# Longformer attention and cosine-gated layers on one Trainium2 core: seven products of quarters for the second layer of tiles 3 to 5, with new step lists

## The chip, the core and the metric

The kernel runs on one core of a Trainium2 chip. A core has TensorE (PE) for matrix products, with its weight loads shown apart (PEld), VectorE (DVE), ScalarE (ACT), GpSimd (POOL) and SyncE (SP), which issues DMAs. Each engine works through its own list of instructions in order, and waits on semaphores that other engines raise. The matrix products land in PSUM, eight banks of 128 partitions x 512 fp32 numbers. The metric is device time in microseconds (us), median over executions. One further execution is recorded by the hardware profiler, and all lines of the profile come from that one.

## What is computed

Attention over 8 batches of 8 heads with 576 positions and 64 numbers per head, where a position sees those at most 32 away, and 8 global positions see all and are seen by all; then two layers with a cosine gate between them.

```python
scores = scale * np.matmul(q, k.transpose(0, 1, 3, 2))
mask = np.abs(pos[:, None] - pos[None, :]) <= window
mask = mask | is_global[:, None] | is_global[None, :]
...
attn = np.exp(scores); attn = attn / (np.sum(attn, axis=-1, keepdims=True) + 1e-09)
x = np.matmul(attn, v).transpose(0, 2, 1, 3).reshape(B * S, H * D)   # 4608 x 512
h = x @ w_in                                                        # 512 x 2048
g = h * np.cos(h)
return g @ w_out                                                    # 2048 x 512
```

Inputs and output are fp32; products take fp16 operands.

## The kernel before

**Attention.** Two heads of one batch make a pair, so there are 32 pairs, four to a batch. A pair goes through these stations: local keys and queries copied beside the global ones (DVE, L630 and L642; the global ones by POOL, L600 and L607), scores (PE, L722, 22 small products into three PSUM banks `s` and one of `h`), exponentials (ACT, L725 for two blocks of 128x512, L730 for two rests of 128x192), mask products (DVE, L726 and L731), values (PE, L742, into `pv`), the division (DVE, L747 to L753), six transposes (PE, L767, into `tx`) and two copies into `xT` (DVE, L769 and L770). `x_squares` (ACT, L914) and, per batch, copies of the global rows (POOL, L775) follow.

**Layers.** The 4608 tokens are nine tiles of 512. A first-layer unit (`mlp_in`, L788) is four 512-column products into one bank `ph`; ACT takes the cosine (L794) and DVE multiplies (L795) into `g`. There are 16 such units to a tile. The second layer of tiles 0 to 5 is done directly: 16 units of four 512-column products (L892), a bank `po` copied out after every four units by ACT (L897) and DVE (L899) in turn, and stored. Tiles 6 to 8 (`WT = 6`) use seven products of quarter matrices in place of eight (`win`, L852): 14 units of eight 256-column products, with sums of quarters of `g` made ahead (`g_sum`, L822, eight DVE instructions of 1024 columns to a tile) and of `w_out` (`w_out_sum`, L808, eight in all), and results collected from two banks X and Y, by ACT copies where a result's first part comes, and DVE additions (L876) where its second does.

**Order.** The program writes each engine's order out by hand: a list of letters is run in sequence, and each letter appends its instructions to the engines. Steps s = 4 to 15 each treat two pairs, `a` (2s) and `z` (2s+1), and copy keys and queries for the next two, `c` and `d`. In a list, `1` is a first-layer unit with cosine and product, `2` a second-layer unit, `sa`/`sz` scores with exponentials and masks, `pa`/`pz` values with division, `xa`/`xz` transposes with their copies, `k.`/`q.` the local copies, `n` the squares, `J` one `w_out_sum`, `G` the casts: POOL copies the four global blocks, waits for the division of `z` through a small gate copy, and then issues three DMAs that write the fp16 v, k and q of step s+2 to DRAM. At the end of a step `bring(s + 2)` puts the transposing loads of keys and queries (SP, L295 and L296) and the value loads on SP's queue. `FRONT`, `MID` (s = 4), `FIFTH`, `SIXTH`, `ORDER` (s = 7 to 14), `LASTR` (s = 15) and `TAIL` are the lists. Each step of `ORDER` has eight `1` and eight `2`.

The two functions of ACT, exp and sine, need different tables; a table load stands before the first exponential and before the first cosine of each step.

Of the kernel before, what the change touches and what calls it, by code (L numbers as in the profile page):

```python
# [51 lines left out]
TAIL = "x0 a4 a5 o x1 a6 i w o i i o o i o w i w a7 o i w i o i v0 b0 o b1 i i o i o b2 i i o o w i w w i b3 o o i w b4 i o i b5 i o b6 w o i o i w o i v1 i o i w w o c0 b7 o i c1 v2 i o c2 i o c3 o i o i i w w o w i o i w o c4 c5 c6 o o c7 o v3 o F o o o o R o o o o o"  # L52
# [3 lines left out]
FIFTH = "sa G 2 2 2 n3 2 sz pa U10 K7 1 1 2 xa pz 2 2 2 kc qc xz n"  # L56

SIXTH = "kz qz sa 2 2 2 2 sz pa 1 2 1 2 xa n pz D0 1 1 G 2 xz 1 D1 1 2 kc qc 1 D2 1"
# [5 lines left out]
WT = 6  # L64
WIN = "1265734"
# [146 lines left out]
def kernel(  # L212
# [20 lines left out]

    ident = const.tile([P, P], FP32)
# [91 lines left out]
    def warm(n, tag="s"):  # L326

        t = ps.tile([P, 4, P], FP32, tag=tag, bufs=2 + (tag == "s"))
        for _ in range(n):
            nc.tensor.matmul(t, ones16, view(ones16, (0, 4), (1, P)), start=True, stop=True)  # L330
# [94 lines left out]
    def value_rows(s, part):  # L425

        hs = slice(2 * part, 2 * part + 2)
        rows = ps.tile([P, 512], FP32, tag="h", bufs=2, name="rows")
# [143 lines left out]
    def turn_globals(half, both):  # L572
        t = ps.tile([P, 2, 16 * G], FP16, tag="s" if half else "h", bufs=2 + half)
# [22 lines left out]
    def globals_k(pr):  # L596
        if pr < 2 * HY:
            nc.gpsimd.tensor_copy(k5(pr)[:, :, 0:G], view(kgT[:, pr], (0, NK5), (1, G)))
            return
        nc.gpsimd.tensor_copy(kw[pr % NK][:, :, 0:G], view(kgT[:, pr], (0, NB), (1, G)))  # L600

    def globals_q(pr):
# [4 lines left out]
        nc.gpsimd.tensor_copy(qp[:, :, 0:G], view(qgT[:, pr], (0, NB), (1, G)))  # L607

    def turned(src, pr, n, ahead=0):

        bank = ps.tile([P, 512], FP32, tag="h", bufs=2, name="bank")
        for _ in range(ahead):
            nc.tensor.matmul(bank, ones16, view(ones16, (0, 4), (1, P)), start=True, stop=True)
        t = view(bank.bitcast(FP16), (QP, RW), (1, QP))
# [4 lines left out]
        return t, bank[:, 400 : 400 + G]  # L619
# [23 lines left out]

    def scores5(pr):
        kp, qp = k5(pr), qb[pr % NK].rearrange("p j c -> p (j c)")
        pm = pm_of[pr] = work.tile([P, 2 * CN], FP16, tag="pm", name="pm")
        tags = (("s", 3), ("s", 3), ("s", 3), ("o", 1))
        st = [ps.tile([P, 512], FP32, tag=tag, bufs=bufs, name="st") for tag, bufs in tags]
# [44 lines left out]
    def turn_x5(pr, tag="s"):  # L693
        b, p = pr // NP, pr % NP
# [4 lines left out]
        tx = ps.tile([P, NK5, P], FP16, tag=tag, bufs=2 + (tag == "s"))  # L699
# [12 lines left out]
    def scores(pr):  # L712
        if pr < 2 * HY:
            return scores5(pr)
        kp, qp = kw[pr % NK], qb[pr % NK]
        pm = pm_of[pr] = view(work.tile([P, 2 * CN], FP16, tag="pm", name="pm"), (NB * C, 2), (C, NB), (1, C))
        tags = (("s", 3), ("s", 3), ("s", 3), ("o", 1) if front[0] else ("h", 2))
        st = [ps.tile([P, 512], FP32, tag=tag, bufs=bufs, name="st") for tag, bufs in tags]
        for j in range(NB):
            for h in range(2):  # L720
                hp = slice(h * D, (h + 1) * D)
                nc.tensor.matmul(st[j // 8 * 2 + h][:, j % 8 * C : j % 8 * C + C], kp[hp, j], qp[hp, j], start=True, stop=True)  # L722
        for h in range(2):
            e = work.tile([P, 2 * CB], FP16, tag="e", bufs=3)
            nc.scalar.activation(e[:, 0:512], st[h], AF.Exp, scale=scale)  # L725
            nc.vector.tensor_tensor(view(pm[:, h], (1, 512)), e[:, 0:512], view(mask, (1, 512)), ALU.mult)  # L726
        e = work.tile([P, 2 * CB], FP16, tag="e", bufs=3)
        n = (NB - 8) * C
        for h in range(2):
            nc.scalar.activation(e[:, h * n : (h + 1) * n], st[2 + h][:, 0:n], AF.Exp, scale=scale)  # L730
        nc.vector.tensor_tensor(view(pm[:, 0, 8], (NB * C, 2), (1, n)), view(e, (n, 2), (1, n)), view(mask[:, 8], (0, 2), (1, n)), ALU.mult)  # L731

    def values(pr):
        if pr < 2 * HY:
            return values5(pr)
        pm, vp = pm_of.pop(pr), vw[pr % NV]
        for j0 in range(0, NB, 2):
            for h in range(2):
                for j in range(j0, min(j0 + 2, NB)):
# [3 lines left out]
                                     start=True, stop=True)  # L743
        den = pv[:, :, D : D + 1]
# [11 lines left out]

    def turn_x(pr):
        if pr < 2 * HY:
            return turn_x5(pr, "h" if 5 < pr < 8 else "s")
        b, p = pr // NP, pr % NP  # L760
        xn = xn_of[pr // 2][:, pr % 2]
        if p == 0:
            xg_of[b] = work.tile([P, NP, G], FP16, tag="xg", name="xg")
        xg = xg_of[b]
        tx = ps.tile([P, BP, P], FP16, tag="s", bufs=3)
        for n in range(BP):
            nc.tensor.transpose(tx[:, n], xn[:, n], ident16)  # L767
# [9 lines left out]
    def mlp_in(t, f):  # L777
# [6 lines left out]
        else:  # L784
            ph = ps.tile([P, TT], FP32, tag=tag, bufs={"s": 3, "h": 2}[tag], name="ph")
# [12 lines left out]
    w_of = [xT[:, :, i * TT : (i + 1) * TT] for i in range(4)]  # L798
# [11 lines left out]
    s_of, wp_of, o_of, o_next = {}, {}, {}, [0]  # L810

    def g_sum(t, k):

        n, part = HF // 4, k // 4
        if t not in s_of:
            s_of[t] = [room[3]] + [xT[:, :, i * TT : (i + 1) * TT] for i in (4, 5)] if t % 2 else room[0:3]
        s1, s2, s4 = (x[:, n * part : n * part + n].rearrange("p a (b n) -> p a b n", n=NH) for x in s_of[t])
# [12 lines left out]
    def win(t, u):  # L830

        name, a = WIN[u // 2], u % 2
        g16, wo = g_of[t], w_out16
        s1, s2, s4 = s_of[t] if t in s_of else (None,) * 3
        half = lambda x, f: x[:, f // 2, f % 2 * NH : f % 2 * NH + NH]
        left = {"1": lambda f: g16[:, f, 0:NH], "2": lambda f: g16[:, HF + f, 0:NH], "3": lambda f: half(s4, f),
                "4": lambda f: g16[:, HF + f, NH:], "5": lambda f: half(s1, f), "6": lambda f: half(s2, f),
# [7 lines left out]
        if name == "1" and (split or a == 0):  # L845
            tag = "h" if split else "o"
            X[at] = ps.tile([P, 2, NH], FP32, tag=tag, bufs={"h": 2, "o": 1}[tag], name="wx")
        if name in "25" and (split or a == 0):
            Y[at] = ps.tile([P, 2, NH], FP32, tag="s", bufs=3, name="wy")
        bank = (X if name in "1674" else Y)[at]  # L850
        for f in range(HF):
            nc.tensor.matmul(bank[:, a], left(f)[:, a * P : a * P + P], right(f),  # L852
# [4 lines left out]
        b = bank[:, cols]  # L857
        if name == "1" and cols.start == 0 or name == "1" and not split:
            o_of[t] = [o_room() for _ in range(4)]
        o11, o12, o21, o22 = (o[:, cols] for o in o_of[t])  # L860
# [4 lines left out]
        if name == "1":  # L865
            nc.scalar.copy(o11, b)
        elif name == "6":
            nc.scalar.copy(o12, b)
        elif name == "5":
            nc.scalar.copy(o22, b)  # L870
        elif name == "4":
            nc.scalar.copy(o21, b)
            store(o21, 1, 0, nc.scalar if split else nc.sync)
        else:
            o, tok, col = {"2": (o11, 0, 0), "3": (o12, 0, 1), "7": (o22, 1, 1)}[name]
            nc.vector.tensor_tensor(o, b, o, ALU.add)  # L876
            if not split or name != "2":
                store(o, tok, col, nc.sync)
            elif a:
                store(o_of[t][0], tok, col, nc.sync)  # L880

    def mlp_out(t, u):
# [4 lines left out]
        if part == 0:  # L887
            tag = "s" if (tail[0] or spare[0]) and s % 2 else "o"
            po_of[t] = ps.tile([P, DM], FP32, tag=tag, bufs={"s": 3, "o": 1}[tag], name="po")
# [37 lines left out]
    def weight_norms(c):  # L927
        sq = w_sq.pop(c)
        pn = ps.tile([P, 512], FP32, tag="s", bufs=3)
# [27 lines left out]
    def raise_flag(count):  # L957
        tot, onesf = count
        pt = ps.tile([P, 512], FP32, tag="o", bufs=1)
# [6 lines left out]
    outs_q = [(t, u) for t in range(NTT) for u in range(NF if t < WT else 2 * len(WIN))]  # L966
# [20 lines left out]
    outs_by = [0]  # L987
# [12 lines left out]
    with tc.manual_schedule():  # L1000
# [36 lines left out]
        pv = ps.tile([P, 2, 512], FP32, tag="pv", bufs=1)  # L1037
# [35 lines left out]
        def casts(s):  # L1073

            for pr in (2 * s + 2, 2 * s + 3):
                if pr < B * NP:
                    globals_kq(pr)
# [8 lines left out]
        def bring(s):  # L1086
# [6 lines left out]
        OTHER = LOCAL | {"g": globals_kq, "L": load_qk, "W": load_w_in, "v": load_values, "n": x_squares,  # L1093
                 "C": cast_vn, "I": row_numbers, "E": early_rows, "w": lambda n: warm(n, "h" if n == 6 else "s"), "y": value_rows, "M": next_values, "S": spread_vg, "V": hold, "N": hold_mask, "U": hold_x, "H": early_globals, "Z": steady_buffers, "f": fill, "r": load_vn, "A": later_rows, "D": later_globals, "O": load_w_out, "K": lambda s: cast_half(s, "kqv"), "B": bring, "J": w_out_sum, "j": lambda k: g_sum(WT, k), "m": lambda _: one(False), "t": lambda _: mlp_act()}
# [8 lines left out]
        for s in range(4, B * NP // 2):  # L1103
            outs_by[0] = 8 * (s - 3)
            for step in {4: MID, 5: FIFTH, 6: SIXTH, 15: LASTR}.get(s, ORDER).replace("J", f"J{s - 7}" if s < 15 else "").split():
# [10 lines left out]
                elif step == "n":  # L1116
                    x_squares(s - 1)
                elif step == "R":
# [75 lines left out]
```

## Time and profile before

| what | value |
|---|---|
| median of three runs | 337.71 us (337.55 to 337.84) |
| the profiled execution | 339.82 us |
| its span | 338.1 us |
| mean granted clock of TensorE | 0.986 |
| DVE, ACT, POOL busy, share of the span | 80%, 71%, 32% |

The span runs from the first to the last instruction of the profiled execution; 1.7 us of that execution lie outside it. A busy share is an average over the whole span: the program has a front of 80 us (loads, the first eight pairs), the steps up to about 266 us, and a tail of tiles 7 and 8. From 76 us to the last slice but one the page's slices show PE at 9 (90% or more). From 300 us on, only layers are left.

### The profile page before, as it was taken

To read this page: it belongs to the slowest core of one execution; us is meant where nothing else is said; L and a number is where in the kernel's file an instruction comes from. 1 tells how busy PE (TensorE), PEld (TensorE's weight loads), DVE (VectorE), ACT (ScalarE), POOL (GpSimd) and SP (SyncE) were. 2 spreads that over 40 slices of the span, in tenths; PEclk is the share of its full clock that TensorE was granted. 3 is DMA by queue.
4 is the path that set the end of the run, shared out by engine and by line. 5 is a ranking of instruction groups with operands and counts; after the bars stand their busy time and mean duration, and the time that the engine had idled before them with its cause. 6 is when DMAs were issued, how large, how long until landed. Compare 5 with 4: busy or idle time off the path is not lost.

```text
span 338.1 us, 8637 instructions
## 1 busy us (share of the span) xinstructions
PE 325.8 (96%) x3269; PEld 182.1 (54%) x3269; DVE 271.8 (80%) x648; ACT 241.6 (71%) x423; POOL 107.2 (32%) x216
## 2 busy tenths in 40 slices
PE   7989989999999999999999999999999999999993
PEld 3567664444445454545454545454545566666682
DVE  6757998996488889889888989898889877778781
ACT  4776886786768787878787878787878775666720
POOL 6856567624061507060805080507000200000000
PEclk9996999999999999999999999999999999999998
DMA  4999899999999999999999999999990000200212
GB/s 74 209 166 179 162 204 202 196 148 149 143 137 180 131 161 146 176 141 172 154 200 139 202 131 185 136 181 148 209 112 34 32 33 0 95 32 0 94 47 86
DMA packets 167203, 45.00 MB, mean 133 GB/s; under 512 B 153092, under 2 KB 163716, under 8 KB 166980
## 3 DMA queue, kind: packets, MB, share of 16 engines
q1 hardware_dynamic: 107396, 26.60, 55.3%
q0 software_dynamic: 59472, 17.54, 53.1%
q8 instruction: 27, 0.44, 0.6%
q10 hardware_dynamic: 288, 0.26, 0.2%
q14 instruction: 20, 0.16, 0.2%
HBM read 44.93 MB, written 19.17 MB: 190 GB/s over the span
## 4 chain that ended last, share of the span: by engine, by line
PE 80%; DVE 7%; ACT 5%; issue 2%; DMA 2%; SPq 2%; POOL 0%; ACTq 0%; DVEq 0%
PE ph L788 27%; PE po L892 21%; PE wx L852 6%; PE wy L852 5%; PE units L788 4%; PE t L330 3%; PE pv L742 3%; PE st L722 2%; DVE g L795 2%; DMA vw<-vg 2%; PE tx L767 2%; PE bank L618 2%; PE pv L669 1%; PE st L654 1%; ACT cos L794 1%
## 5 line engine op out<-in xcount | busy, mean ns | idle before, releaser
L788 PE MATMUL ph<-xT,w_in 128*128 128x512 f16 x512 | 123.3, 379 | 0.4
L794 ACT ACTIVATE cos<-ph,pio 128x512 f16<-128x512 f32 x128 | 86.4, 686 | 41.9 <-PE ph L788 39.9
L795 DVE TENSOR_TENSOR g<-cos,ph 128x512 f16<-128x512 f16 x128 | 85.6, 683 | 18.0 <-ACT cos L794 16.2
L892 PE MATMUL po<-w_out,g 128*128 128x512 f16 x384 | 93.5, 379 | 0.0
L788 PEld LDWEIGHTS <-w_in 128*128 128x128 f16 x576 | 53.9, 98 | 57.5 <-issue 1.5
L892 PEld LDWEIGHTS <-g 128*128 128x128 f16 x384 | 36.6, 98 | 43.1
L725 ACT ACTIVATE e<-st 128x512 f16<-128x512 f32 x44 | 23.9, 594 | 8.2 <-PE st L722 8.1
L726 DVE TENSOR_TENSOR pm<-e,mask 128x512 f16<-128x512 f16 x44 | 18.8, 427 | 13.4 <-ACT e L725 12.1
L1079 POOL COPY gate<-xn 1x1 f16<-1x1 f16 x8 | 1.4, 179 | 81.4 <-DVE xn L753 81.4
L775 POOL COPY xT<-xg 128x4 f16 x48 | 15.9, 331 | 32.0 <-DVE xT L770 29.4
L281 POOL DMA_DIRECT2D q<-in_q_dram x11 | 24.3, 2206 | 0.0
L753 DVE TENSOR_TENSOR xn<-pv,r_all 128x768 f16<-128x768 f32 x22 | 21.1, 958 | 0.7
L852 PEld LDWEIGHTS <-g 128*128 128x128 f16 x192 | 18.7, 98 | 5.2
L914 ACT ACTIVATE xn<-xn 128x1536 f16<-128x1536 f16 (+1 forms) x15 | 21.2, 1411 | 0.0
L281 POOL DMA_DIRECT2D k<-in_k_dram x11 | 18.0, 1638 | 1.4 <-issue 1.4
L794 ACT ACTIVATE cos<-units,pio 128x512 f16<-128x512 f32 x16 | 11.0, 688 | 9.8 <-PE units L788 9.6
L795 DVE TENSOR_TENSOR g<-cos,units 128x512 f16<-128x512 f16 x16 | 11.0, 686 | 7.4 <-ACT cos L794 7.2
L788 PE MATMUL units<-xT,w_in 128*128 128x512 f16 x64 | 16.4, 379 | 0.0
L794 ACT ACT_TABLE_LOAD x12 | 15.4, 1283 | 0.2
L657 ACT ACTIVATE e<-st 128x488 f16<-128x488 f32 x20 | 10.4, 572 | 6.4 <-PE st L654 6.4
L725 ACT ACT_TABLE_LOAD x11 | 14.1, 1283 | 0.2
L600 POOL COPY kw<-kgT 128x88 f16<-128x88 f16 x22 | 14.0, 858 | 0.0
(214 smaller groups left out, 505.8 us busy)
## 6 DMA issues: line engine op xcount, KB each, us to landing
out_dram<-o SPq DMA_DIRECT2D x24, 256.0 KB
vw<-v SPq DMA_DIRECT2D x32, 165.0 KB
k<-in_k_dram POOLq DMA_DIRECT2D x11, 288.0 KB, 8.2
q<-in_q_dram POOLq DMA_DIRECT2D x11, 288.0 KB, 10.7
v<-in_v_dram POOLq DMA_DIRECT2D x11, 288.0 KB, 5.5
vn<-in_v_dram SPq DMA_DIRECT2D x20, 120.0 KB
w_in<-in_moe_w_in_dram POOLq DMA_DIRECT2D x4, 512.0 KB, 9.3
w_out<-in_moe_w_out_dram POOLq DMA_DIRECT2D x1, 2048.0 KB, 17.0
```

What stands on the lines that cost most here:

```text
L281: nc.gpsimd.dma_start(dst[s].rearrange("t (h d) -> t h d", h=4), dview(src, base, (D, S), (S * D, 4), (1, D)))
L600: nc.gpsimd.tensor_copy(kw[pr % NK][:, :, 0:G], view(kgT[:, pr], (0, NB), (1, G)))
L725: nc.scalar.activation(e[:, 0:512], st[h], AF.Exp, scale=scale)
L726: nc.vector.tensor_tensor(view(pm[:, h], (1, 512)), e[:, 0:512], view(mask, (1, 512)), ALU.mult)
L753: nc.vector.tensor_tensor(view(xn, (384, 2), (D, 6), (1, D)), view(pv, (512, 2), (65, 6), (1, D)), view(rp, (6, 2), (1, 6), (0, D)), ALU.mult)
L775: nc.gpsimd.tensor_copy(xT[:, :, bass.ds(pool_idx[g] + b * S, 1)], xg[:, :, g : g + 1])
L788: nc.tensor.matmul(ph, w_in16[:, j, f * P : (f + 1) * P], xT[:, j, t * TT : (t + 1) * TT], start=(j == 0), stop=(j == NC - 1))
L794: nc.scalar.activation(cos, ph, AF.Sin, bias=pio2)
L795: nc.vector.tensor_tensor(g, cos, ph, ALU.mult)
L852: nc.tensor.matmul(bank[:, a], left(f)[:, a * P : a * P + P], right(f), start=name in "125" and f == 0 and (split or a == 0), stop=f == HF ...
L892: nc.tensor.matmul(po, g16[:, f, s * P : (s + 1) * P], w_out16[:, f], start=(f == 0), stop=(f == NF - 1))
L914: nc.scalar.activation(view(xn, (BP * P, 2), (1, n)), view(xn, (BP * P, 2), (1, n)), AF.Square, accum_out=x_sq[:, s : s + 1])
```

## The change

1. **`WT = 3`:** tiles 3 to 5 take the seven products too, in the order 1, 2, 6, 7, 5, 3, 4. Their sums of `g` lie in columns of `xT` whose tokens are used up (`g_rooms`), the sums of `w_out` in `room`, made by `J0` to `J7` in steps 6 to 9, where before they came one a step in 7 to 14. Each of these tiles' outputs leaves as four quarters `oq`, four ACT copies and three DVE additions to a tile, in place of two ACT and two DVE copies.
2. **Banks:** the pools of PSUM become one tile `banks` of all eight banks, with a fixed ring for each purpose. From step 4 on, both score pairs of a step write banks 0, 1 and 2 (and one of the `h` banks 4 and 5). Transposes take banks 2 and 0 in turn; X of the seven products is bank 3 and Y bank 1.
3. **Smaller letters:** scores with exponentials (`e`), masks (`h`), values (`b`), division (`d`), transposes (`l`) and their copies (`u`) can be placed apart. The two 128x512 exponentials become one of 128x2x512 that writes `pm` at once; the masks are multiplied in place, 128x2x512 and 128x2x192.
4. **Tables:** `load_table` is a 1x1 ACTIVATE whose only use is that the table is loaded there: sine after the odd pair's exponentials, exp at the letter `P`.
5. **Globals:** for pairs 12 and up ACT, not POOL, copies the global keys and queries (`yc`, `yd`), four to a step.
6. **Lists:** `FIFTH` and `SIXTH` are rewritten, steps 7, 8 and 9 get lists of their own with eight `1` and eight `2` each, and from 10 on `EVEN` (six `1`, of them one as `m` and `t`, and five `2`) and `ODD` (ten and nine) alternate; step 15 has a new `LASTR`. `m` is a first-layer unit whose cosine and product wait for the letter `t`.

```diff
-ORDER = "2 kz qz sa 2 2 2 sz pa 1 2 1 2 xa n pz 1 1 G J 2 xz 1 1 2 kc qc 1 1"
-LASTR = "2 kz qz sa 2 2 2 sz pa 1 j0 2 1 2 xa n pz 1 1 j1 2 xz 1 j2 1 2 1 j3 1"
+SEVENTH = "2 kz ea qz 2 J4 2 ez ha 2 ba hz da 1 2 J2 1 bz dz la ua yd 2 n 1 G 1 2 lz uz kc 1 1 qc yc 2 1 1 J3"
...
+NINTH = "kz 2 ea qz 2 ha yc 2 2 ez hz ba da 1 2 1 2 n la ua bz yd dz 1 1 G 2 lz j0 J7 uz 1 1 qc kd kc 2 1 j1 1 qd"
+EVEN = "ea j4 2 j3 ha ez j5 m hz ba da t 2 kc 1 2 yd bz dz 1 1 la n ua 2 G yc qc 1 1 P lz uz j7 2 qd kd"
+ODD = "2 ea j2 2 ha j6 ez hz 2 ba da 1 1 2 bz la dz 1 1 ua G n 2 qd lz 1 1 yc 2 j0 uz 1 1 yd 2 kc 1 qc m 2 t P kd j1 2"
+LASTR = "2 ea j2 2 ha j6 ez hz 2 ba da 1 1 2 bz la dz 1 1 ua n 2 lz 1 1 2 j0 uz 1 1 2 2 1 2 j1 1"
...
-WT = 6
-WIN = "1265734"
+WT = 3
+WIN = "1265734", "1267534"
...
+    banks = ps.tile([P, 8, 512], FP32, tag="banks", bufs=1, name="banks")
+    rings, turns = {"s": [0, 1, 2], "o": [3], "h": [4, 5], "t": [2, 0], "y": [1]}, {}
...
+    def score_banks(pr):
+        return [bank(tag) for tag in "ssso"] if front[0] else [banks[:, i] for i in (0, 1, 2)] + [bank("h")]
...
+            nc.scalar.activation(both, banks[:, 0:2], AF.Exp, scale=scale)
...
+        if not front[0] and pr % 2:
+            load_table(AF.Sin)
+    def mask_scores(pr):
...
+        nc.vector.tensor_tensor(both, both, view(mask, (0, 2), (1, 512)), ALU.mult)
+        nc.vector.tensor_tensor(rest, rest, view(mask[:, 8], (0, 2), (1, n)), ALU.mult)
...
-        nc.gpsimd.tensor_copy(kw[pr % NK][:, :, 0:G], view(kgT[:, pr], (0, NB), (1, G)))
+        (nc.scalar.copy if pr > 11 else nc.gpsimd.tensor_copy)(kw[pr % NK][:, :, 0:G], view(kgT[:, pr], (0, NB), (1, G)))
...
+    def g_rooms(t, part):
+        if t < 6:
+            c = column((t if part else t - 2) % NTT)
+            return c[:, 0:2], c[:, 2:4], c[:, 2:4]
```

**Scores at a step's start.** On ACT, before, a step of `ORDER` begins behind the cosines of the last step (`cos`) with the table load (the kernel's L725) and the exponentials of `a` and `z`; on PE three second-layer units stand between the two pairs' scores.

```order
L794 ACTIVATE cos<-ph,pio_71 128x512 x2
L725 ACT_TABLE_LOAD
L725 ACTIVATE e<-st 128x512 x2
L730 ACTIVATE e<-st 128x192 x2
L725 ACTIVATE e<-st 128x512 x2
L730 ACTIVATE e<-st 128x192 x2
```

After, from step 11's end into step 12, the table load of `P` and its 1x1 instruction come ahead of a copy out of bank X (`oq<-banks`), and that copy ahead of the exponentials, which now write the masked products' place `pm`.

```order
L854 ACTIVATE cos<-banks,pio_72 128x512 x2
L746 ACT_TABLE_LOAD
L746 ACTIVATE table<-pio_72 1x1
L943 COPY oq<-banks 128x512
L762 ACTIVATE pm<-banks 128x2x512
L764 ACTIVATE pm<-banks 128x192 x2
L762 ACTIVATE pm<-banks 128x2x512
```

The copy, which frees bank X for the next second-layer unit, moved to the step's first place on ACT, and a cosine's table is left a unit earlier. On PE the same place reads, with waits: the last of one second-layer unit's products (L923), then the first scores of `z` (L756) with the semaphore of ACT, `Activation_49`.

```order
L923 LDWEIGHTS g
L923 MATMUL banks<-room_90,g 128x256
L756 LDWEIGHTS kw_100 [waits DVE_49]
L756 MATMUL banks<-qb_104,kw_100 128x64 [waits Activation_49]
L756 LDWEIGHTS kw_100
L756 MATMUL banks<-qb_104,kw_100 128x64
```

One unit of eight products stands there between the scores of `a` and of `z` in the steps of `EVEN` and `ODD`, where three units of four stood; `z` writes the banks that `a` wrote.

**DVE in a step.** Before, a step begins with the masks, a copy out of `po` between them, and the division.

```order
L726 TENSOR_TENSOR pm<-e,mask 128x512 x2
L731 TENSOR_TENSOR pm<-e,mask 128x2x192
L899 COPY o<-po 128x512
L726 TENSOR_TENSOR pm<-e,mask 128x512 x2
L731 TENSOR_TENSOR pm<-e,mask 128x2x192
L747 TENSOR_REDUCE dg<-pv 8x2
```

After, in a step of `EVEN`, sums of quarters (L892) stand ahead of and between the masks.

```order
L892 TENSOR_TENSOR xT<-xT,g 128x2x512
L892 TENSOR_TENSOR xT<-g 128x2x512
L892 TENSOR_TENSOR g<-g 128x4x256
L772 TENSOR_TENSOR pm<-pm,mask 128x2x512
L773 TENSOR_TENSOR pm<-pm,mask 128x2x192
L892 TENSOR_TENSOR xT<-xT,g 128x2x512
L772 TENSOR_TENSOR pm<-pm,mask 128x2x512
L773 TENSOR_TENSOR pm<-pm,mask 128x2x192
L797 TENSOR_REDUCE dg<-banks 8x2
```

The first of these sums ends the step of `ODD` before, the other three belong to `EVEN`; a tile's eight sums of 1024 columns are spread four to a step of either kind, where before there was one sum of `w_out` to a step. The copy out of `po` is gone from between the masks.

More of the change, by code (lines that the diff above doesn't have):

```diff
@@ L427, in value_rows @@
         hs = slice(2 * part, 2 * part + 2)
-        rows = ps.tile([P, 512], FP32, tag="h", bufs=2, name="rows")
+        rows = bank("h")
         for t in range(NK5):
@@ L797 @@
     NH, HF = DM // 2, NF // 2
-    w_of = [xT[:, :, i * TT : (i + 1) * TT] for i in range(4)]
+    w_of = room
     def w_out_sum(k):
```

174 lines of the change are left out of this document (98 added, 76 removed).

## Prediction

> **What bounds the kernel now.** I read the page's busy table first, then windows of 20 us, since a share over the whole span mixes stages.
>
> ```profile
> 80.00:100.00 20.00, 18.98 (x193) 9.39 (x192) 12.69 (x30) 13.12 (x22) 4.29 (x6) 1.00 1.40 153
> 120.00:140.00 20.00, 20.00 (x220) 10.37 (x220) 17.68 (x41) 15.88 (x26) 6.73 (x16) 1.00 1.55 164
> 200.00:220.00 20.00, 20.00 (x201) 10.01 (x199) 17.14 (x38) 16.39 (x27) 6.88 (x16) 1.00 1.70 159
> 240.00:260.00 20.00, 20.00 (x205) 10.34 (x204) 17.59 (x38) 16.12 (x26) 0.00 (x0) 1.00 0.89 113
> ```
>
> The columns are the window, its length, then busy us of PE, PEld, DVE, ACT and POOL, the granted clock, the DMA share and GB/s. In the steps PE is busy 20.00 of 20 at a clock of 1.00: PE is the bound, DVE follows at 86 to 88%, ACT at 80%. Only the window that holds step 5 leaves PE idle, 1.02 us. The timeline gives the period:
>
> ```profile
> 116.94 0.49 PE L722 MATMUL st<-qb,kw 64*128 64x64 f16 x22
> 117.37 2.76 PE L892 MATMUL po<-w_out,g 128*128 128x512 f16 x12
> ...
> 124.45 0.50 PE L767 MATMUL tx<-ident,xn 128*128 128x128 f16 x6
> 124.88 0.57 PE L742 MATMUL pv<-vw,pm 128*64 128x65 f16 x22
> ...
> 127.98 0.50 PE L767 MATMUL tx<-ident,xn 128*128 128x128 f16 x6
> 128.32 1.89 PE L788 MATMUL ph<-xT,w_in 128*128 128x512 f16 x8
> ...
> 133.59 0.49 PE L722 MATMUL st<-qb,kw 64*128 64x64 f16 x22
> ```
>
> From one step's first scores to the next's: 133.59 - 116.94 = 16.65 us, 33.3 for two steps, in which one tile passes both layers.
>
> **A. What the products save.** The chain of waits has whole units of both kinds (start, length, matmuls):
>
> ```profile
> 149.45 0.86 PE po L892 x4
> ...
> 287.11 1.75 PE wy L852 x16
> ```
>
> A direct unit takes 0.86 us; a unit of the seven products 1.75 / 2 = 0.875. A tile falls from 16 x 0.86 to 14 x 0.875, by 1.5 us, or by 1.6 with 0.863, which part B's rows give for three units (251.01 to 253.70, less 0.10 for entering scores); three tiles by **-4.7 us**. PE has no idle time to hide it, so all of it counts.
>
> **B. What the new order of scores costs.** Both pairs now write banks 0 to 2, and in `EVEN` and `ODD` one unit lies between them, so z's first score waits for a's merged exponential. Before, three units covered it:
>
> ```profile
> 249.62 1.03 PE L892 MATMUL po<-w_out,g 128*128 128x512 f16 x4
> 249.82 0.69 ACT L794 ACTIVATE cos<-ph,pio 128x512 f16<-128x512 f32 x1 [0.18 <-PE ph L788]
> ...
> 250.53 1.28 ACT L725 ACT_TABLE_LOAD   x1
> ...
> 250.58 0.49 PE L722 MATMUL st<-qb,kw 64*128 64x64 f16 x22
> ...
> 251.01 2.76 PE L892 MATMUL po<-w_out,g 128*128 128x512 f16 x12
> 251.82 1.09 ACT L725 ACTIVATE e<-st 128x512 f16<-128x512 f32 x2
> ...
> 253.70 0.49 PE L722 MATMUL st<-qb,kw 64*128 64x64 f16 x22
> ```
>
> Scores occupy PE for 0.43 (250.58 to 251.01); entering them from a unit costs 0.96 - 0.86 = 0.10. The load starts 0.02 after the cosine ends and the exponential 0.01 after the load: nothing but 1.28 stands between. z's scores came at 253.70, long after the exponentials (252.91). The merged exponential and what stands ahead of it on ACT:
>
> ```profile
> L725 ACT ACTIVATE e<-st 128x512 f16<-128x512 f32 x44 | 23.9, 594 | 8.2 <-PE st L722 8.1
> L730 ACT ACTIVATE e<-st 128x192 f16<-128x192 f32 x44 | 12.4, 345 | 0.0
> L897 ACT COPY o<-po 128x512 f32<-128x512 f32 x12 | 7.0, 585 | 6.3 <-PE po L892 6.3
> L638 ACT COPY qb<-bank 128x8 f16<-128x8 f16 x10 | 2.0, 200 | 0.2 <-PE bank L618 0.2
> ```
>
> From 345 ns at 192 columns to 594 at 512 is 0.778 ns a column, so 1024 columns take 594 + 512 x 0.778 = 0.99 us; 0.80 without fixed cost and 1.09, the pair above, are the ends. The tiny instruction behind a load I price as the 8-column copy, 0.20. Let T be the start of a's scores; PE is ready for z at T + 0.43 + 0.875 + 0.10 = T + 1.40.
> - Steps 11, 13, 15: the copy out of bank X starts T + 0.20 (its unit ends at T), hands ACT on after 0.48 (an estimate: 0.585 less the 0.1 by which the pair of 594 overlaps), the exponential runs T + 0.68 to T + 1.67, z starts 0.06 later: wait 0.33. Three make 1.0.
> - Steps 12, 14: behind `m`, whose end is T - 1.75, stand its cosine to T - 0.86, the load to T + 0.43, the tiny instruction to T + 0.63, the copy to T + 1.1, the exponential to T + 2.1: wait 0.75. Two make 1.5.
> - Step 10 has no `P` before it: the last unit's cosine to T + 0.89, the load to T + 2.18, the exponential to T + 3.17: wait 1.8.
>
> Behind the waiting score the whole of PE's list is queued, and DVE waits for PE; so B is **+4.3 us**. Its ends: a longer exponential adds 0.1 to each of six waits, and if ACT runs 0.75 ahead of this they all go but 1.1 of step 10's: +1.1 to +4.9. I take the worked value, since each piece of it has a row.
>
> The Trainium skill, page "ScalarE: Activation LUTs", section "What ACT_TABLE_LOAD costs", adds a drain of about 1380 ns to the 1283 ns of every switch of table sets. Here the cosine's end and the exponential lie 1.31 us apart, so this trace shows no drain; with one, three waits of B would grow by 1.38 each, and the sum by 4.1.
>
> **C. Entering values.** Before, a's values came behind z's scores or behind transposes; now a's and z's come behind units. Transposes pass to values in 0.43 (124.45 to 124.88) and to a unit in 0.34 (127.98 to 128.32), so only one new entry of 0.1 a step is left; steps 5, 7 and 10 to 15 have it: **+0.8** (0 to 1.6).
>
> **D. Steps 5 to 7.** Step 5's stalls in the timeline:
>
> ```profile
> 86.86 0.26 PE L722 MATMUL st<-qb,kw 64*128 64x64 f16 x6 [0.33 <-ACT o L897]
> ...
> 91.54 2.12 PE L788 MATMUL ph<-xT,w_in 128*128 128x512 f16 x8
> ...
> 99.14 0.67 PE L722 MATMUL st<-qb,kw 64*128 64x64 f16 x22 [0.62 <-DVE qb L642]
> ```
>
> The first two go with bank 3 no longer under scores and with the new list, the last with `kz`, `qz` set earlier: 0.33 + 0.22 (2.12 against 1.90) + 0.62 = 1.2 go, and new ones of 0.5 for step 5's two late transposes I estimate; in steps 6 and 7 cosine, load and exponential stand before values and z's scores as in step 10, but a unit earlier and behind two units: 0.2 each by the same working. Together **-0.3** (-1.2 to +0.6).
>
> **E. Small ones.** DVE's and ACT's own prices:
>
> ```profile
> L731 DVE TENSOR_TENSOR pm<-e,mask 128x384 f16<-128x384 f16 x22 | 7.9, 358 | 0.5
> L726 DVE TENSOR_TENSOR pm<-e,mask 128x512 f16<-128x512 f16 x44 | 18.8, 427 | 13.4 <-ACT e L725 12.1
> L822 DVE TENSOR_TENSOR room<-g 128x1024 f16<-128x1024 f16 x6 | 4.1, 686 | 0.0
> L876 DVE TENSOR_TENSOR vw<-wy,vw 128x512 f32<-128x512 f32 x2 | 1.4, 692 | 0.6 <-PE wy L852 0.6
> L899 DVE COPY o<-po 128x512 f32<-128x512 f32 x12 | 8.3, 691 | 2.5 <-PE po L892 1.8
> L600 POOL COPY kw<-kgT 128x88 f16<-128x88 f16 x22 | 14.0, 858 | 0.0
> ```
>
> The globals' copies, 0.86 on POOL, lie on ACT between 0.20 (8 columns) and 0.345 (192): four make 1.1 a step. ACT, 16.4 of 20 or 13.6 a step, goes to about 15.3 with two more copies of 0.585 in two steps, inside 16.4: hidden, and if ACT's cover were gone they would delay cosines by 1.1 a step. POOL gets free, which ends nothing. `m` and the units behind it wait for banks now and then: +0.3 (0 to 0.9). Keys and queries are turned by SP:
>
> ```profile
> 211.05 0.18 POOL L1079 COPY gate<-xn 1x1 f16<-1x1 f16 x1 [9.08 <-DVE xn L753]
> 220.17 2.30 SPq L295 DMA_TRANSPOSE kT<-k  x1
> 224.47 2.10 SPq L296 DMA_TRANSPOSE qT<-q  x1
> ...
> 167.65 7.42 DMA vw<-vg
> ```
>
> They land at 226.6, 15.5 after the gate and 9.7 into the step; `qd` in `ODD` now stands some 10.6 into it, where the list before had its first use at its end: +0.4 (0 to 1.8). The last row is of the chain: a value load held step 10; with units in other places perhaps 0.2 of it goes, and 0.3 at the end of step 15 where the exponential's bank was late: -0.5 (-1 to 0).
>
> **The sum:** -4.7 + 4.3 + 0.8 - 0.3 + 0.3 + 0.4 - 0.5 = +0.3 us, made against the profiled execution (339.82, of which the span is 338.1): 340.1. That execution lies 2.1 above the median of the runs, 337.71; carried over, the time is **338.0 us**. A measurement tells about 0.2% (0.7 us) from no change.
>
> **Rivals.**
> 1. *The saving stays.* If ACT reaches the exponentials sooner, B shrinks to step 10's wait, and C to nothing: -4.7 + 1.1 - 0.1 = -3.7, **334.0 us**. For it: ACT is busy 80% only, so that it may come to a step's start earlier than I let it; against it: its copy out of X and the exponential cannot start before PE has ended what they read.
> 2. *DVE becomes the bound (slower).* Two steps hold 17.2 / 20 x 33.3 = 28.6 us of DVE now. Added are 8 x 0.686 of sums and 3 x 0.69 of additions, taken away two copies of 0.69, two `w_out` sums of 0.69 and 0.6 of masks (a column costs 0.54 ns by the two mask rows, so a pair's 2 x 0.427 becomes 0.70, four times): 32.8 us, where PE wants 33.3 - 1.6 + 1.1 = 32.8. It decides from a DVE share of 98%: then masks and divisions come late to values and transposes, about 1.0 us in two steps if DVE is behind by one sum and one small mask (0.69 + 0.36), three times, or **341.0 us**. Against it: neighbours in a full queue overlap, so that busy sums fall when DVE is pressed; two products that take 0.683 each apart take 1.28 together:
>
> ```profile
> L795 DVE TENSOR_TENSOR g<-cos,ph 128x512 f16<-128x512 f16 x128 | 85.6, 683 | 18.0 <-ACT cos L794 16.2
> ...
> 94.62 1.28 DVE L795 TENSOR_TENSOR g<-cos,ph 128x512 f16<-128x512 f16 x2 [0.19 <-ACT cos L794]
> ```
>
> 3. *The transposed queries are late.* `qd` waits 0.9 in steps 11 and 13, and DVE's list behind it: 1.4 more than in the sum, **339.4 us**.
> 4. *The clock.* The windows from 40 us on have a clock of 1.00, that of step 5 too, in spite of its 1.02 us of idle PE; in the front another was lower:
>
> ```profile
> 20.00:40.00 20.00, 18.58 (x370) 13.01 (x367) 16.23 (x47) 14.75 (x36) 9.65 (x23) 0.83 1.04 178
> ```
>
> If PE's many short waits brought 0.83 into one such window, it would cost 20 x 0.17 = 3.4: **341.4 us**. The Trainium skill, page "TensorE: Matmul & The Clock Gate", section "A second HAM failure mode: psum-queue depth-cycling", has such idles between groups of matmuls with cycling banks make the clock oscillate; in the windows above it did not.
> 5. *A drain behind each table load:* +4.1, **342.1 us**; the row of B speaks against it.
>
> **Chances.** Forecast 0.40 (own range 336.5 to 339.5: 0.09 faster, 0.21 same, 0.10 slower); the saving stays 0.24; DVE 0.24 (0.02 of it same); queries 0.08 (0.02 same); clock 0.03; drain 0.01. So faster 0.33, same 0.25, slower 0.42. The range leaves out a third of the second case and about half of the third and the last two: 334.2 to 341.2.
>
> **What will show it.** A: units of eight products at 0.875 in steps 10 to 15. B: rows of scores with an idle time put down to ACT's `pm`, 0.3 in odd, 0.75 in even steps, 1.8 in step 10; waits under 0.15 would prove rival 1. DVE above 98% in those windows, with PE waiting for DVE, shows rival 2; `qb` copies waiting for the transposing load, rival 3; a clock under 1.00 after 80 us, rival 4. I would be wrong altogether if steps 5 to 9 changed by more than 1 us.

## The result and the profile after

The changed kernel takes 346.78 us (median of 6, 345.31 to 350.15) against 337.63 us before in the same comparison (6, 335.7 to 338.42): a ratio of **1.029, 95% interval 1.023 to 1.034**. The forecast was 338.0, the range to 341.2. Ratios here compare undisturbed executions only, medians are over all. The profiled execution is the fastest of the six, 345.31, with a span of 343.4. The two profiled executions differ by 5.5 us where the medians differ by 9.2; what made the other executions of the changed kernel longer the profile does not show.

The windows of the changed kernel (columns as in the prediction):

```profile
140.00:160.00 20.00, 20.00 (x185) 10.13 (x184) 17.36 (x40) 16.09 (x30) 5.07 (x7) 1.00 1.54 153
160.00:180.00 20.00, 16.34 (x177) 9.51 (x175) 17.20 (x38) 14.93 (x27) 7.72 (x14) 1.00 1.53 146
180.00:200.00 20.00, 16.19 (x186) 10.50 (x185) 15.28 (x34) 13.15 (x24) 5.21 (x6) 0.97 1.63 147
200.00:220.00 20.00, 19.41 (x207) 12.73 (x205) 17.80 (x38) 16.40 (x31) 5.42 (x12) 0.95 1.18 144
220.00:240.00 20.00, 19.23 (x228) 12.82 (x228) 18.89 (x40) 16.19 (x32) 5.56 (x12) 1.00 1.67 158
```

PE is idle for 7.5 us between 160 and 200 us, in steps 10 and 11, and DVE and ACT are less busy there than next door, so neither is the bound there. The times between the first scores of `a` in one step and another, from the timelines (the right column is run e12, below):

| steps | before | after | e12 |
|---|---|---|---|
| start to the first scores of 5 | 86.12 | 83.97 | 88.67 |
| 5, 6 | 30.82 | 29.08 | 29.06 |
| 7 | 16.65 | 18.33 | 16.81 |
| 8, 9 | 33.39 | 32.70 | 32.70 |
| 10, 11 | 33.65 | **41.91** | 34.66 |
| 12, 13 | 33.30 | 32.88 | 33.23 |
| 14 to the end | 104.17 | 104.53 | 103.47 |

Steps 10 and 11 alone cost 8.3 us more than before; 12 and 13, with the same two lists, are 0.4 shorter than before, as the forecast's sum of A, B and C for two steps (-1.6, +1.1 and +0.2) would have it. The first row is the front, whose lists `FRONT` and `MID` the change leaves alone: it differs from one execution to the next, with a granted clock of 1.00 (after), 0.83 (before) and 0.66 (e12) in the window from 20 to 40 us. From step 5 to the end the changed kernel's profile is 7.45 us longer than before. The chain of waits in steps 9 to 11 of the changed kernel (start, length, what) names the way:

```profile
157.49 0.97 DVE xn L803
...
158.59 0.18 POOL gate L1144
...
159.54 9.07 DMA k<-in_k_dram
...
168.62 5.86 DMA kT<-k
...
174.50 0.54 DVE kw L650
...
176.12 0.97 DVE xn L803
...
177.14 0.18 POOL gate L1144
...
178.96 11.37 DMA q<-in_q_dram
...
190.34 6.66 DMA qT<-q
```

A division lets a gate pass, the casts go to DRAM, SP's transposes turn them, a copy takes them up, and the next step's division hangs on that copy. The timeline shows what waits on DVE and then on PE (in brackets the idle time and who ended it):

```profile
174.50 0.54 DVE L650 COPY kw<-kT 128x1320 f16<-128x1320 f16 x1 [1.87 <-DMA kT<-k]
...
197.02 0.47 DVE L662 COPY qb<-qT 128x616 f16<-128x616 f16 x1 [3.76 <-DMA qT<-q]
...
198.14 3.09 PE L848 MATMUL banks<-xT,w_in 128*128 128x512 f16 x8 [3.62 <-DVE g L855]
201.02 1.56 PE L923 MATMUL banks<-w_out,xT 128*128 128x256 f16 x8
202.42 1.89 PE L848 MATMUL banks<-xT,w_in 128*128 128x512 f16 x8
```

DVE stands at the copy, the products `g` queued behind it come late, and PE waits 3.62 us for a bank that such a product must read first; behind the copy of step 10 it waits 1.97 in the same way. Then the clock falls: the same eight products take 3.09 us at 198.14 and 1.89 at 202.42, and eight of 256 columns 1.56 where others take 1.04. Windows of one microsecond from 198 to 203 show a granted clock of 0.84, 0.50, 0.50, 0.50 and 0.96, which costs 1.7 us. The two waits and the clock make 7.3 us, and steps 10 and 11 are 7.25 longer than in e12, which has none of the three.

From gate to landed keys are 15.9 us (158.59 to 174.50), to landed queries 19.9 (177.14 to 197.02). `EVEN`'s `kc` asked 14.0 after the gate, `ODD`'s `qd` 16.1. Before, `kc` and `qc` at the end of a step asked some 21 after it.

### The profile page after: what moved, and what is told of

Its sections match the earlier page's. It is cut to its first block, busy times and chain, and to the rows that moved or that the text cites. A ratio compares the mean times of both kernels' runs of the same rounds, so it can differ in the third digit from the quotient of the medians.

```text
span 343.4 us, 8941 instructions
## 1 busy us (share of the span) xinstructions
PE 321.3 (94%) x3413; PEld 194.4 (57%) x3413; DVE 277.9 (81%) x653; ACT 249.2 (73%) x463; POOL 95.1 (28%) x176
## 4 chain that ended last, share of the span: by engine, by line
PE 61%; DMA 11%; ACT 11%; DVE 10%; issue 4%; POOL 1%; SPq 0%; ACTq 0%; DVEq 0%; POOLq 0%
PE banks L848 26%; PE banks L923 15%; PE banks L960 9%; DVE g L855 4%; DMA kT<-k 3%; DMA q<-in_q_dram 3%; DMA k<-in_k_dram 3%; ACT cos L854 2%; PE banks L350 2%; DMA qT<-q 2%; PE banks L756 2%; DVE kw L650 2%; PE banks L789 1%; ACT L746 1%; PE banks L692 1%
## 5 line engine op out<-in xcount | busy, mean ns | idle before, releaser
L848 PE MATMUL banks<-xT,w_in 128*128 128x512 f16 x576 | 138.2, 382 | 8.2 <-DVE g L855 7.7
L854 ACT ACTIVATE cos<-banks,pio 128x512 f16<-128x512 f32 x144 | 97.0, 684 | 58.5 <-PE banks L848 54.1
L855 DVE TENSOR_TENSOR g<-cos,banks 128x512 f16<-128x512 f16 x144 | 95.9, 683 | 22.7 <-ACT cos L854 20.5
L960 PE MATMUL banks<-w_out,g 128*128 128x512 f16 x192 | 46.6, 379 | 0.0
L923 PEld LDWEIGHTS <-g 128*128 128x128 f16 x384 | 36.8, 98 | 10.1 <-issue 1.1
L923 PEld LDWEIGHTS <-xT 128*128 128x128 f16 x288 | 28.4, 99 | 7.8 <-issue 0.5
L923 PE MATMUL banks<-w_out,g 128*128 128x256 f16 x192 | 23.9, 273 | 1.2 <-ACT oq L943 1.2
L923 PE MATMUL banks<-room,g 128*128 128x256 f16 x192 | 24.4, 273 | 0.4
L762 ACT ACTIVATE pm<-banks 128x1024 f16<-128x1024 f32 x22 | 22.5, 1021 | 2.8 <-PE banks L756 2.0
L923 PE MATMUL banks<-room,xT 128*128 128x256 f16 x192 | 23.6, 273 | 0.0
L803 DVE TENSOR_TENSOR xn<-banks,r_all 128x768 f16<-128x768 f32 x22 | 21.1, 958 | 0.7
L756 PEld LDWEIGHTS <-kw 64*128 64x128 f16 x484 | 8.7, 95 | 9.1 <-issue 5.0
```

What stands on the lines that cost most here:

```text
L762: nc.scalar.activation(both, banks[:, 0:2], AF.Exp, scale=scale)
L803: nc.vector.tensor_tensor(view(xn, (384, 2), (D, 6), (1, D)), view(pv, (512, 2), (65, 6), (1, D)), view(rp, (6, 2), (1, 6), (0, D)), ALU.mult)
L848: nc.tensor.matmul(ph, w_in16[:, j, f * P : (f + 1) * P], xT[:, j, t * TT : (t + 1) * TT], start=(j == 0), stop=(j == NC - 1))
L854: nc.scalar.activation(cos, ph, AF.Sin, bias=pio2)
L855: nc.vector.tensor_tensor(g, cos, ph, ALU.mult)
L923: nc.tensor.matmul(xy[:, a], left(f)[:, a * P : a * P + P], right(f), start=name in "125" and f == 0 and (split or a == 0), stop=f == HF - ...
```

## The experiments

Labels are short: e1 is the run e1_late_copies, and so on. All but the base of a diff is the changed kernel's.

**Asking later (e1, e2), casting earlier (e3).**

```diff
-EVEN ... da t 2 kc 1 2 ... G yc qc        +EVEN ... da t 2 1 2 ... G yc kc qc      (e1)
-ODD ... n 2 qd lz ... P kd j1 2           +ODD ... n 2 lz ... P kd qd j1 2         (e1, e2)
-nc.gpsimd.tensor_copy(gate, xn_of[s][0:1, 1, 0, 0:1])
+nc.gpsimd.tensor_copy(gate, xn_of[s][0:1, 0, 0, 0:1])                              (e3)
```

> Theory (the transposed keys and queries land after the place where EVEN's kc and ODD's qd now ask for them, VectorE's list stands still behind the copy, and TensorE waits for the products of cosines behind it): with kc moved behind yc in EVEN and qd moved to the end of ODD, the waits of kw for kT (1.9 and 1.1 us) and of qb for qT (3.8 us) are gone, the gap from step 11's to step 12's first scores falls from 24.2 to about 19 us, and the time is 339 to 341 us, ratio 1.00 to 1.01. Rival (VectorE is the bound in steps 10 to 15, or the waits of z's scores are the whole loss): the time stays at 345 to 347 us, ratio 1.025, with VectorE above 95% in the windows from 160 to 260 us.

> Only qd of ODD is moved to the end of the step; kc of EVEN stays early. Theory: the largest wait (3.8 us at step 11) goes, those of kw for kT stay: 342 to 343.5 us, ratio about 1.015, between the changed kernel and the run with both moved. Rival: 345 to 347 us.

> Lists as in the changed kernel, but the gate that paces the casts waits for the division of the step's first pair in place of its second, so that the casts start about 3 us earlier. Theory: kT and qT land about 3 us earlier, the waits of 1.9 and 1.1 us go and that of 3.8 us falls under 1: 340 to 342 us, ratio 1.007 to 1.013. Rival (transposes are late only because the step itself is late): 345 to 347 us, the transposes as late as before.

Measured: e1 341.21 us, ratio 1.014 (1.010 to 1.017); e2 344.74, 1.024 (1.020 to 1.029); e3 343.28 with executions from 340.0 to 351.6, 1.016 (1.009 to 1.023). Two moved letters give back 5.6 of the 9.2 us: the lateness of keys and queries is the main cause. The rival (DVE or z's scores alone) falls as the main cause. e1 came out 0.2 us above what I expected, e2 and e3 1.2 and 1.3. In e1 no copy waits for a DMA, yet steps 12 and 13 take 36.0 us, and the reason is another. POOL's issues and DVE's copy of keys in step 12 of e1, and PE at the start of step 13:

```profile
210.50 2.19 POOL L301 DMA_DIRECT2D q<-in_q_dram  x1
...
210.88 2.16 DVE L650 COPY kw<-kT 128x1320 f16<-128x1320 f16 x1
...
215.26 0.50 PE L756 MATMUL banks<-qb,kw 64*128 64x64 f16 x22 [1.82 <-DVE xT L830]
```

A `kw` copy that takes 0.53 elsewhere takes 2.16 beside POOL's issue of a cast, and ends 0.35 after it; the turned values behind it free a score's bank 1.8 us late. Behind that wait, too, the clock falls to 0.50 for about 3.4 us (1.7 us lost). In the changed kernel the same happened in step 7:

```profile
125.42 2.64 DVE L650 COPY kw<-kT 128x1320 f16<-128x1320 f16 x1
125.58 2.48 POOL L301 DMA_DIRECT2D q<-in_q_dram  x1
```

Both end at 128.06. The Trainium skill, page "SBUF — State Buffer", section "Who interferes with whom", says that a DVE copy in a two-port mode and GpSimd hold one shared pair of ports in turn, each for a whole instruction; the 2.64 us in place of 0.53 agree with that, though the page's example has the DMA waiting for the copy. Which mode this copy runs in, no run here shows.

**The order of the casts (e4), casts a step ahead (e5).**

```diff
-cast_half(s + 2, "vkq")
+cast_half(s + 2, "kqv")                                  (e4)
+if s == 6: cast_half(8, "vkq")
+cast_half(s + 3, "vkq")                                  (e5, for s = 6 to 12)
```

> Lists as in the changed kernel; only the order of the three casts behind the gate is k, q, v in place of v, k, q. Theory (keys and queries reach kT and qT too late, because a cast of keys takes 9 us from its issue and one of queries 11, behind that of values): k lands some 3 us sooner, q some 2, so the waits of kw for kT (1.9 and 1.1 us) go and that of qb for qT (3.8 us) falls to under 2: 341 to 343.5 us, ratio 1.010 to 1.018. Rival (the transposes stand in SP's queue behind value loads, whatever the casts do): 345 to 347 us, the transposes issued no earlier than before.

> Lists as in the changed kernel; each step's casts are those of step s+3 in place of s+2 (step 6 issues both its own and the next). Theory: keys and queries lie in DRAM a whole step before their transposes, which then are issued at once at a step's end; no copy waits for kT or qT, two steps take 32.9 us as steps 12 and 13 of the changed kernel do, and the time is 335.5 to 338 us, ratio 0.995 to 1.003. Rival (VectorE or the order of scores sets the period, transposes only fill it): over 343 us. Rival (SP's queue holds the transposes back): 340 to 345 us, with kT issued over 3 us behind the step's end though k has landed.

Both missed: e4 347.11, ratio 1.025 (1.020 to 1.030); e5 347.08, 1.031 (1.023 to 1.039). In e4 the waits of `kw` for kT are 2.7 and 3.4 us, while the queries' wait falls from 3.8 to 0.5. Before the first of them the cast keys lie in DRAM 8.7 us after their gate, in place of 10.0, but their transposing load takes 8.0 us to land, in place of 5.9. Before the second, SP issues that load only at 210.25, 6.2 us into the step, behind loads of values and three stores of `oq`: there e4's rival holds. In e5 the waits shrink to 0.7 to 1.2, and step 9 to the end takes 190.2 us against 195.4; but step 6 issues the casts of two steps, step 7 takes 18.5 us, and step 8, where values wait 1.45 and 0.66 us for their small loads and 1.7 us go to the clock, takes 20.7.

**Out of POOL's way (e6, e7), and the globals (e8).**

```diff
-SEVENTH ... uz kc 1 1 qc yc 2 1 1 J3      +SEVENTH ... uz 1 1 qc yc 2 kc 1 1 J3   (e6, e7; both on e1)
-EVEN ... G yc kc qc ... lz uz j7          +EVEN ... G yc qc ... lz uz kc j7       (e7)
-(nc.scalar.copy if pr > 11 else nc.gpsimd.tensor_copy)(...)
+nc.gpsimd.tensor_copy(...)                                                        (e8, on the changed kernel)
```

> The run with EVEN's kc and ODD's qd late, and besides the kc of SEVENTH moved from right behind uz to behind one more first-layer and one second-layer unit. Theory (a kw copy that comes while POOL issues the step's three casts stands until the last of them is issued; in step 7 of the changed kernel one took 2.64 us for 0.53, and in EVEN of the run with late copies 2.06 and 2.16): step 7's copy takes 0.53 us, step 8's first scores come 1 to 2 us sooner, 339 to 340.5 us against 341.2. Rival (the long copy is hidden, or comes from elsewhere): no change, 341.

> As the run before of this call, but EVEN's kc stands behind uz, after POOL's casts are issued and long after kT has landed. Theory: both mechanisms are gone, every kw copy takes 0.53 us and waits for nothing; two steps take 33 us or a little more in place of 36, 336 to 338.5 us, ratio 0.997 to 1.004. Rival (VectorE's own load, 33.6 us busy in two steps, sets the period whatever the copies meet): two steps stay above 34.5 us and the time at 340 or above.

> The changed kernel with one part undone: POOL copies all global keys and queries again, at the places yc and yd. Theory: nothing on TensorE's path hangs on who makes them, save that POOL's copies stand in one list with the casts; 345.5 to 349 us, ratio 1.023 to 1.035. Rival (ScalarE's 80 more copies press its list, cosines come late, and part of the loss is there): 343 us or less.

Measured: e6 343.72 us, 1.016 (1.009 to 1.024); e7 341.02 with executions from 338.8 to 346.2, 1.005 (1.001 to 1.009); e8 348.27, 1.030 (1.022 to 1.037). e6 and e7 missed. In e6 step 7 does fall, from 18.3 to 16.8 us, and the time does not. Its profile gives no reason: from step 5 to the end it is 1.4 us shorter than e1's, with 1.5 more in step 11 and 1.5 less in step 13 (no fall of the clock there); its front is 2.4 longer. In e7 every `kw` copy takes 0.5 and waits for no DMA, and now values are late, in step 13 of its profile, which is of an execution of 345.89 us, 4.9 above e7's median, so that this wait may not be in most:

```profile
223.05 0.80 PE L789 MATMUL banks<-vw,pm 128*64 128x65 f16 x22 [2.53 <-DMA vw<-vg]
```

With the clock's 1.7 us behind it this wait is the whole of what step 13 takes beyond e12's (22.9 to 18.7). e8 shows that who copies the globals does not matter, as expected.

**The control, and casts ahead once more (e9 to e11).** e10 changes the kernel *before* by one letter.

```diff
-MID ... 2 2 kc qc n1 ...  FIFTH ... bz K7 yd ...
+MID ... 2 2 kc qc V10 K7 n1 ...  FIFTH ... bz K8 yd ...  cast_half(s + 3)     (e9 on e7; e11 on the changed lists, with e6's SEVENTH)
-ORDER = "... xa n pz 1 1 G J 2 xz 1 1 2 kc qc 1 1"
+ORDER = "... xa kc n pz 1 1 G J 2 xz 1 1 2 qc 1 1"                            (e10, on the kernel before)
```

> The lists of the run with EVEN's kc at its end, and each half's casts one step earlier from step 5 on (step 4 gets a gate of its own and casts half 7, step 5 casts half 8, step s from 6 on casts half s+3), so that no step issues two. Theory (the way from a step's gate over casts, SP's queue of transposes and value loads to the first use is what the uneven steps run into: keys first, then values behind them in the same queue): kT, qT and value loads are issued at once at a step's end, no copy and no value product waits for a DMA, two steps take 32.5 to 33.5 us, and the time is 334.5 to 337.5 us, ratio 0.990 to 1.000. Rival (VectorE's load or the order of scores sets the period): two steps over 34 us with value products waiting for VectorE, 339 us or more.

> The kernel before with one letter moved: kc of steps 7 to 14 from behind xz and a unit to right behind xa, some 6.5 us earlier in the step. Theory (keys land 15 to 17 us after a step's gate, which stands about 10.5 us into it, so that a copy at 8 us into the next step of 16.65 comes 1 to 3 us before they land): VectorE waits for kT in most of these steps and stands, and the time rises by 4 to 15 us, to 342 to 353. Rival (the late transposes of the changed kernel come from its banks, copies or stores, not from when they are asked for): under 339.5 us.

> EVEN and ODD as in the changed kernel (kc and qd early), with the casts one step ahead as in the first run of this call and the kc of SEVENTH moved out of POOL's casts. Theory: kT is issued at the step's end with its keys long in DRAM and lands some 8 us later, near where EVEN asks (8.5 us into the step); waits of 0.5 to 1 us remain in some steps, 336 to 340 us, ratio 0.995 to 1.008. Rival: as the changed kernel, 344 to 347.

Measured: e10 344.34 us, 1.016 (1.009 to 1.023): the old kernel, asked for its keys 5.8 us sooner (8.8 in place of 14.6 into a step), loses 6.3 us by the medians, with the same waits (`kw` for kT 0.54, 0.75 and 2.03 us in its profile, the last with a fall of the clock to 0.50). e9 347.26, 1.029 (1.025 to 1.034), and e11 346.89, 1.027 (1.023 to 1.032), missed: the added cast makes step 5's queries 5.6 and 8.7 us late, and the clock is at 0.50 behind that for 7 and 10 us. From step 9 to the end both take 188.9 us, close to the 187.9 before and 6.5 less than the changed kernel, e11 with `EVEN` and `ODD` as they were. So the later steps can be mended by earlier casts, and the price is paid where the cast is put in.

**What fills the way (e12 to e15).** SP's issues take up 30.0, 28.4 and 24.8 us of three windows of 30 from 150 to 240 in the kernel before (sums of its timeline's lengths), and 29.4, 30.1 and 28.1 in e9; in the changed kernel itself they take 22.6, 23.0 and 24.5, since SP waits there for casts to land. e12 and e13 leave out the loads of the global tokens' values for pairs 20 to 31, so older rows stand there.

```diff
 def load_vg(pr):
-    for h in range(2): nc.sync.dma_start(vw[pr % NV][0:G, :, h, 0:D], ...)
+    for h in range(2 if pr < 20 else 0): ...                       (e12 on e7; e13 on the kernel before)
+    for h in range(2): (nc.scalar if pr > 19 else nc.sync).dma_start(...)   (e14 on e7; e15: nc.gpsimd)
```

> The lists of the run with EVEN's kc at its end, without the two small loads (vw<-vg, 11 KB each) of the global tokens' values for pairs 20 to 31; those pairs use older rows there, so 24 DMAs are left out and nothing else. Theory (SP's queue is taken up by its issues nearly all the time, and transposes and value loads come late to the uneven steps because they stand behind one another in it): the loads' 3 us a step are gone from the queue, kT is issued and values land that much sooner, no value product of ODD waits for a DMA, two steps take 33 to 33.5 us in place of 35.6 and 37.4, and the time is 334.5 to 338 us, ratio 0.990 to 1.000. Rival (the data's way, not the queue, is full; 22 KB a pair are nothing in it): 339.5 to 342 us, with the same waits of values in ODD.

> The kernel before without the same 24 loads of the global tokens' values (pairs 20 to 31 use older rows there). Theory (its even steps get keys and values in time, TensorE is the bound): no change but the one stall of step 10, 336.5 to 338.5 us, ratio 0.995 to 1.002. Rival (SP's queue holds every kernel back, this one too): under 335.5 us.

> The lists with EVEN's kc at its end, nothing left out; the 24 loads for pairs 20 to 31 are issued by ScalarE in place of SP, four at the end of each step. Theory: SP's queue is as free as without them, but ScalarE, which a step's first exponential waits for, spends their issue time there (0.8 us each on SP, so up to 3 a step): 338 to 344 us; if an issue costs ScalarE little, 336 to 338. Rival (the queue was not the cause): values late as before, 340 to 342 us with waits of value products for DMAs.

> As the run before, with GpSimd issuing the 24 loads, behind each step's casts. Theory: SP's queue is free, GpSimd has time, the value products of ODD do not wait for a DMA; only a kw copy that meets these issues can grow by up to 2 us, since one step's copies follow right behind them: 336 to 340 us, ratio 0.995 to 1.007. Rival (the queue was not the cause): 340 to 342 us with values late as before.

Measured: e12 339.35 us (336.5 to 343.7), 1.001 (0.998 to 1.005); e13 336.78, 0.997 (0.994 to 1.000); e14 384.56, 1.139 (1.132 to 1.146); e15 343.22, 1.016 (1.010 to 1.021). Only e13 came out within its range; e12 lies 1.4 us above, e15 3.2, e14 41. Scores of `a` in steps 12 to 14 of e12:

```profile
201.90 0.49 PE L756 MATMUL banks<-qb,kw 64*128 64x64 f16 x22
...
216.45 0.50 PE L756 MATMUL banks<-qb,kw 64*128 64x64 f16 x22 [0.49 <-DVE kw L650]
...
235.13 0.49 PE L756 MATMUL banks<-qb,kw 64*128 64x64 f16 x22
```

With 24 loads fewer in SP's queue no copy and no product of these steps waits for a DMA, the clock stays at 1.00, and two steps take 33.23 us; e13 says that the old kernel hardly gains from the same. The wait of 0.5 us in these rows, which steps 11 and 15 have too, is for DVE. In e14 ACT's next copies and exponentials stand behind its own DMA issues:

```profile
205.11 0.69 ACTq L455 DMA_DIRECT2D vw<-vg  x1
205.85 0.59 ACT L943 COPY oq<-banks 128x512 f32<-128x512 f32 x1 [7.96 <-DMA kT<-k]
```

ACT's waits for DMAs add up to 37 us there, the longest 10.2, and PE's clock is at 0.50 for some 44 us. In e15 values are late again (1.6 us in step 9, 2.6 in step 11); both waits are for loads that SP issued, and why they were late these rows do not say. Whether SP's time for issues or the DMA engines' work is what is full these runs do not tell apart, and no whole kernel that beats both came of them.

## Why the prediction was wrong, step by step

- **E's term for keys and queries is the step that failed**: +0.4 (0 to 1.8) for what cost 7 to 8 us in the profile. First, it misread the landing. "They land at 226.6" is 224.47 + 2.10, the end of SP's issue of the transposing load, and the data land later. The changed kernel shows both views of one load, the issue here and the load itself (6.66) in the chain above:

```profile
190.34 1.94 SPq L316 DMA_TRANSPOSE qT<-q  x1
```

  With 6.66 in place of 2.10 the forecast's own row gives 231.1, 20.1 after the gate and 13.9 into the step (19.9 after the gate were measured), and `qd`, 10.6 into it, would wait about 3.3; in step 11 it waited 3.76. Second, it left out `kc` in `EVEN`, which waits 1.9 and 1.1 us in steps 10 and 14. Third, it counted the copy's wait alone, and neither DVE's list behind it, nor the lateness handed to the next gate, nor the clock behind PE's wait.
- **Rival 3 named the way**, at 339.4 us and a chance of 0.08, with the same landing in its price. e1 and e10 show it from both sides: -5.6 us by asking later, +6.3 in the old kernel by asking sooner.
- **Rival 4 came with it.** Its sign, a clock under 1.00 after 80 us, is there: 0.97 and 0.95 in the two windows from 180 to 220, 1.7 us. But a long wait stands ahead of the fall, and not many short ones: e12 has B's waits and 1.00 from 80 to 260 us. (That the clock of the kernel before was 1.00 from 40 us on overlooks its last window, 320 to 338, with 0.93.) Rival 5 was no matter: 0.01 to 0.02 us lie between a load of `load_table` and its instruction.
- **Rival 2 is not the cause, but DVE is near.** In `EVEN` steps DVE is busy for 13.67 of 14.12 us (step 12 after) and 13.98 of 14.55 (e12), 96 to 97%, and in e12 the scores of `a` wait 0.5 us for its copy of keys in steps 11, 13 and 15. With DMAs on time two steps still take 32.88 to 33.23 us.
- **A was right.** A unit of the seven products takes what it was given; from the chain after:

```profile
268.42 1.75 PE banks L923 x16
```

- **B was nearly right in size, and its mechanism holds in step 10 alone.** Scores of `a` and of `z`, and what stood between, in steps 10, 12 and 13 after:

```profile
167.19 0.50 PE L756 MATMUL banks<-qb,kw 64*128 64x64 f16 x22 [1.25 <-ACT pm L762]
...
205.99 0.49 PE L756 MATMUL banks<-qb,kw 64*128 64x64 f16 x22
207.07 1.03 PE L923 MATMUL banks<-w_out,g 128*128 128x256 f16 x8 [0.58 <-ACT oq L943]
208.04 0.49 PE L756 MATMUL banks<-qb,kw 64*128 64x64 f16 x22
...
220.11 0.50 PE L756 MATMUL banks<-qb,kw 64*128 64x64 f16 x22
220.75 1.03 PE L923 MATMUL banks<-room,g 128*128 128x256 f16 x8
221.71 0.49 PE L756 MATMUL banks<-qb,kw 64*128 64x64 f16 x22
```

  The gap, 1.40 without a wait, is 2.05 in step 12 and 1.60 in step 13: 0.65 and 0.20 for a forecast 0.75 and 0.33. In step 10, whose `a` began at 164.08, it is 3.11: 1.7 for 1.8. Together some 3.6 for 4.3. In step 10 z's scores wait for the exponential (`pm`), as forecast. In steps 12 and 13 the time stands ahead of the unit between (207.07, 220.75), which the forecast let start at once: it needs bank X, and ACT's copy out of X ends just before it, at 207.02 and 220.70. z's scores then follow the unit without a wait.
- **C** fits but no row isolates it: -0.4 in steps 12 and 13 leaves 0.3 beside A's -1.6 and B's 0.85, for a forecast of 0.2.
- **D came out near its sum by luck.** Steps 5 and 6 gain 1.7 us where the forecast's terms give 0.5, and step 7 loses 1.7 where they give 0.2. Moving one `kc` away from POOL's issue takes 1.5 off step 7 (e6), and no term held that; of POOL the forecast said only that it "gets free, which ends nothing".
- **The forecast's 338 is about what is left without the lateness**: e12, at 1.001 (0.998 to 1.005), with A's gain and B's waits and without the loads it leaves out, which are worth some 0.3% in the old kernel (e13).

## What to carry to other kernels

Before moving a consumer, follow its operand back to the event that let its transfer start, through every queue in between, and compare that distance in time, not a place in the step, with the transfer's measured length. Where the slack is a few us in a step, making steps uneven spends it, though the mean period stays. And read a transfer's length to its landing, not to the end of its issue.

## What was not expected of the hardware

- A 128x1320 copy of 0.53 us on DVE took 2.0 to 2.6 us when it came while GpSimd issued a cast (DMA), and ended with that issue (step 7 after) or 0.35 after it (steps 10 and 12 of e1).
- After waits of PE of 3.62 us (after), 1.8 (e1, e10) and 2.5 (e7) the granted clock was 0.50 for about 3.4 us, at a cost of 1.7 us each time; after waits of 1.97 (step 10 after) and 1.83 (e6) it stayed at 1.00. What decides it these runs do not show.
- Small DMA issues are not free on an engine that computes: four a step on ACT cost 43 us in e14 beside e7, with 37 us of ACT's waits for DMAs and 22 of lost clock in its profile.
- A transposing load of one step's keys or queries takes 3.9 to 8.9 us from issue to landing in the chains of the changed kernel, e4, e5 and e10, though SP's issue of it ends after 1.3 to 4.3.
